# The order of the last two multiplications in a rational activation on Trainium2

## The chip, the cores and the metric

The kernel runs on one core of a Trainium2 chip. The core has five engines that run side by side, each taking its own instructions in order: TensorE (matmuls, PE in the profile, with its weight loads as PEld), VectorE (DVE), ScalarE (ACT), GpSimd (POOL) and SyncE (SP), which here issues the DMAs. The engines wait for each other by semaphores. Operands lie in SBUF or in PSUM, where the matmuls write; PSUM has eight banks. The metric is the device time of one execution in microseconds, less is better.

## The reference

Three layers, one after the other. The first is a linear attention with a decay: for each of 4 x 8 heads a 48 x 48 state is carried over 768 time steps. Its output, 3072 tokens of 384 numbers, goes through two feed-forward layers with 2048 hidden units. The change touches the first of them, whose activation is a rational function of the hidden value h:

```python
h = x @ w_in
h2 = h * h
h3 = h2 * h
P = a[0] + a[1] * h + a[2] * h2 + a[3] * h3
Q = 1.0 + np.abs(b[0]) * np.abs(h) + np.abs(b[1]) * h2
g = P / (Q + 1e-06)
return (g @ w_out).astype(np.float32)
```

The second layer has the same form with `g = h * np.cos(h)`.

## The kernel before, in words

The weights arrive as 64-bit floats and are turned into 32-bit ones on the chip (ScalarE L72 and L73, VectorE L77 and L78). Every matmul operand is split into a high and a low part, and a product takes three passes (high by high, high by low, low by high). The order of the work is written out by hand: the program calls the helpers below in the order in which each engine is to run its instructions.

The first part of the run, up to about 105 us, is the attention, in 24 units. The first feed-forward layer overlaps its end. A tile of that layer is 128 hidden units by 512 tokens, and there are 6 x 16 = 96 tiles. The second layer follows with 32 tiles of the same kind, and then its remaining blocks of tokens by a scheme that saves multiplications (`threes`).

`layers(n)` is one step. It runs, in this order: `gemm1(n)`, nine matmuls of tile n into a PSUM bank (L562); `rational(n)`, one stage each for the four tiles before; `second(n)`, the nine matmuls L578 of the tile five before, which need the split activation; and small pieces of other work: the conversion of weights, and the splitting of the next block's input (`x_lo`, VectorE L706, reads two SBUF tiles). The 18 matmuls of a step take about 4.2 us.

The banks of the hidden values go round: tile n uses bank n mod 4 (`b0`, `b1`, `b2`, `r0`; the profile calls them b and r). So `gemm1(n)` can start only when the last reader of tile n - 4 is done.

`rational(n)` does the following. For tile n - 4 ScalarE rounds g to its high part (L608) and GpSimd subtracts to get the low part (L613). For tile n - 1 ScalarE makes |h| (L636) and a linear function of h (L637), GpSimd makes z = |h| (c1 |h| + c0) in two instructions (L638, L639), and VectorE multiplies g by h (L640). For tile n - 2 VectorE does the next step of the polynomial (L628), and ScalarE computes a first guess r of the reciprocal of the scaled denominator, as exp(-ln(...)), in two instructions (L645, L646) and writes it over h in the tile's PSUM bank. For tile n - 3 VectorE corrects the guess by one Newton step and multiplies (L631 to L633). So VectorE has five instructions a step, in the order L628, L631, L632, L633, L640. Of their large operands z and g lie in SBUF, h and r in PSUM.

Of the kernel before, what the change touches and what calls it, by code (L numbers as in the profile page):

```python
# [15 lines left out]
ALU = mybir.AluOpType  # L16
# [15 lines left out]
LN_S = 2.0 ** -22  # L32
# [10 lines left out]
def attn_then_two_moe(ctx, tc, kqT, aT, vP, w1i, w1o, ma, mb, w2i, w2o, out):  # L43
    nc = tc.nc
# [51 lines left out]
    def temp(tag, dtype=F32, shape=(128, TB)):  # L96

        bufs = {"z": 3, "ah": 2, "g": 4, "hi": 3, "lo": 3}[tag]
        return el.tile(list(shape), dtype, tag=tag, name=tag, bufs=bufs)
# [486 lines left out]
    def acc_out(most=NK):  # L586

        while outs and most:
            most -= 1
            m, blk, f, k = outs.pop(0)  # L590
            ks = slice(k * 128, (k + 1) * 128)
            if f < NF - 1:
                nc.scalar.activation(out=part(blk, k), in_=acc[k], func=AF.Copy)
                continue
            o = temp("z" if k == 1 else "g") if m or blk == NC - 1 else in_p.tile([128, TB], F32, tag="p", name="o")
            if in_parts(m, blk):
                nc.vector.tensor_tensor(out=o, in0=part(blk, k), in1=acc[k], op=ALU.add)
            elif m == 1 and k == 1 and blk in (0, NC - 1):
                nc.vector.tensor_copy(o, acc[k])
            else:  # L600
                nc.scalar.activation(out=o, in_=acc[k], func=AF.Copy)
            to = xd[1][blk, ks, :] if m == 0 else out[ks, blk * TB:(blk + 1) * TB]
            nc.sync.dma_start(out=to, in_=o)

    def round_g(n):
        t = T[n]
        t["hi"] = temp("hi", F32R)
        nc.scalar.activation(out=t["hi"], in_=t["g"], func=AF.Copy)  # L608

    def rest_g(n, eng):  # L610
        t = T[n]
        t["lo"] = temp("lo", F32R)
        eng.tensor_tensor(out=t["lo"], in0=t["g"], in1=t["hi"].bitcast(F32), op=ALU.subtract)  # L613

    def rational(n):

        def tile_at(i):
            return T[i] if 0 <= i < N1 else None

        one, two, three, four = (tile_at(n - i) for i in range(1, 5))  # L620
        acc_out(1)
        if four:
            round_g(n - 4)
            rest_g(n - 4, nc.gpsimd)
        acc_out()
        if two:
            g = two["g"]
            nc.vector.scalar_tensor_tensor(g, g, cq[:, 3:4], two["h"], ALU.add, ALU.mult)  # L628
        if three:
            z, r, g = three["z"], three["h"], three["g"]  # L630
            nc.vector.scalar_tensor_tensor(z, z, ONE_EPS, r, ALU.add, ALU.mult)  # L631
            nc.vector.scalar_tensor_tensor(r, z, -2.0 / LN_S, r, ALU.add, ALU.mult)  # L632
            nc.vector.scalar_tensor_tensor(g, g, cq[:, 2:3], r, ALU.add, ALU.mult)  # L633
        if one:
            h, ah, g, zz = one["h"], temp("ah"), temp("g"), temp("z")
            nc.scalar.activation(out=ah, in_=h, func=AF.Abs)  # L636
            nc.scalar.activation(out=g, in_=h, func=AF.Identity, scale=cq[:, 5:6], bias=cq[:, 4:5])  # L637
            nc.gpsimd.tensor_scalar(zz, ah, cq[:, 1:2], cq[:, 0:1], ALU.mult, ALU.add)  # L638
            nc.gpsimd.tensor_tensor(out=zz, in0=zz, in1=ah, op=ALU.mult)  # L639
            nc.vector.tensor_tensor(out=g, in0=g, in1=h, op=ALU.mult)  # L640
            one.update(z=zz, g=g)
        if two:

            r = two["h"]
            nc.scalar.activation(out=r, in_=two["z"], func=AF.Ln, scale=LN_S, bias=lnb)  # L645
            nc.scalar.activation(out=r, in_=r, func=AF.Exp, scale=-1.0)  # L646
# [581 lines left out]
    def layers(n):  # L1228
# [12 lines left out]
        elif n < 2 * NF:  # L1241
            at, load = n - 2 * NF + 4, n == 2 * NF - 6
        split = 0 <= at < NK and nxt[0] < 2 and nxt != (1, 2)
        rational(n)
        cosine_parts(n)
        cosine(n)
# [280 lines left out]
```

## Time and profile before

| What | us |
|---|---|
| median of three runs (913.3 to 915.9) | 914.39 |
| the profiled execution | 913.8 |
| its span, first to last instruction | 912.1 |
| TensorE matmuls busy | 892.4 |
| TensorE weight loads busy | 741.2 |
| GpSimd busy | 702.9 |
| ScalarE busy | 697.1 |
| VectorE busy | 693.9 |

The granted TensorE clock was 0.996 of full speed over the span. Shares of busy time are averages over stages; the table of stages below tells more. An instruction's record runs from its start to its end, and when it is held up after its start by something other than a semaphore, the record becomes longer. In the chain of work that ended last TensorE has 72%, VectorE 8%, ScalarE 7% and GpSimd 6%.

### The profile page before, as it was taken

The numbers are of one execution on the slowest core, as the hardware profiler recorded it, in microseconds if no ns is written. First come the engines' busy times: TensorE is split into PE (matmuls) and PEld (weight loads), VectorE is DVE, ScalarE is ACT, GpSimd is POOL, SyncE is SP. The second block draws the span as 40 slices with busy tenths as digits, with TensorE's granted clock in tenths as the row PEclk, the third lists the DMA queues.
The fourth block names the chain that finished last, engine by engine and source line by source line (L and its number), as shares of the span: only waits on it lengthen the run. The fifth ranks groups of instructions, "written<-read, shape, count | busy, mean of one in ns | idle before, by whom it ended". The sixth has DMA issues, their size and how long they took to land.

```text
span 912.1 us, 16494 instructions
## 1 busy us (share of the span) xinstructions
PE 892.4 (98%) x5732; PEld 741.2 (81%) x5732; DVE 693.9 (76%) x1247; ACT 697.1 (76%) x1302; POOL 702.9 (77%) x699
## 2 busy tenths in 40 slices
PE   7999999999999999999999999999999999999997
PEld 7788777887788888888888888878888888888885
DVE  7989799998999989989979767666366554555552
ACT  5999898989889788888788778656577666666653
POOL 6899998999889888889879668669787475655332
PEclk9999999999999999999999999999999999999999
DMA  8999545211233141232165276630243433533432
GB/s 281 357 366 370 191 124 196 82 63 36 104 107 94 57 142 45 87 107 94 53 205 185 95 238 239 202 110 27 74 134 109 161 113 96 167 102 105 139 105 90
DMA packets 67307, 128.87 MB, mean 141 GB/s; under 512 B 6928, under 2 KB 30224, under 8 KB 67216
## 3 DMA queue, kind: packets, MB, share of 16 engines
q1 hardware_dynamic: 67216, 127.74, 43.1%
q8 instruction: 47, 0.77, 0.4%
q14 instruction: 44, 0.36, 0.1%
HBM read 95.21 MB, written 32.51 MB: 140 GB/s over the span
## 4 chain that ended last, share of the span: by engine, by line
PE 72%; DVE 8%; ACT 7%; POOL 6%; DMA 4%; issue 2%; SPq 0%; DVEq 0%; ACTq 0%
PE acc L578 22%; PE b L562 18%; PE acc L1054 15%; PE b L1019 6%; PE r L1019 5%; PE r L562 4%; POOL kq L323 2%; POOL kq L318 2%; DMA kq<-kqT 2%; DVE g L628 1%; DVE z L631 1%; ACT b L645 1%; DVE g L640 1%; DMA a<-aT 1%; PE b L1198 1%
## 5 line engine op out<-in xcount | busy, mean ns | idle before, releaser
L578 PE MATMUL acc<-hi,w 128*128 128x512 f32 x738 | 252.5, 396 | 0.0
L562 PE MATMUL b<-x,w 128*128 128x512 f32 x927 | 233.8, 397 | 1.3 <-DVE g L633 1.1
L613 POOL TENSOR_TENSOR lo<-g,hi 128x512 fp32r<-128x512 f32 x128 | 170.2, 1330 | 66.2 <-ACT hi L608 59.4
L562 PEld LDWEIGHTS b<-x,w 128*128 128x128 f32 x927 | 173.4, 188 | 45.4 <-DVE g L633 4.1
L578 PEld LDWEIGHTS acc<-hi,w 128*128 128x128 f32 x738 | 138.7, 188 | 33.9
L1111 POOL TENSOR_TENSOR lo<-g,hi 128x512 fp32r<-128x512 f32 x64 | 83.0, 1297 | 103.6 <-ACT hi L1110 91.6
L578 PE MATMUL acc<-lo,w 128*128 128x512 f32 x369 | 145.7, 395 | 0.0
L639 POOL TENSOR_TENSOR z<-z,ah 128x512 f32<-128x512 f32 x96 | 124.7, 1299 | 8.0
L1054 PE MATMUL acc<-hi,w_out 128*128 128x512 f32 x384 | 130.3, 395 | 0.0
L608 ACT ACTIVATE hi<-g 128x512 fp32r<-128x512 f32 x128 | 80.4, 628 | 47.8 <-PE acc L578 32.6
L578 PEld LDWEIGHTS acc<-lo,w 128*128 128x128 f32 x369 | 69.4, 188 | 16.5
L638 POOL TENSOR_SCALAR z<-ah,cq 128x512 f32<-128x512 f32 x96 | 74.4, 775 | 5.5 <-ACT ah L636 5.4
L1054 PE MATMUL acc<-lo,w_out 128*128 128x512 f32 x192 | 76.4, 398 | 0.4 <-POOL lo L1111 0.2
L1054 PEld LDWEIGHTS acc<-hi,w_out 128*128 128x128 f32 x384 | 68.7, 188 | 9.9
L640 DVE TENSOR_TENSOR g<-g,b 128x512 f32<-128x512 f32 x72 | 49.1, 682 | 16.2 <-ACT g L637 16.0
L636 ACT ACTIVATE ah<-b 128x512 f32<-128x512 f32 x72 | 42.8, 594 | 19.9 <-PE b L562 19.6
L562 PE MATMUL r<-x,w 128*128 128x512 f32 x225 | 56.8, 397 | 1.0 <-DVE g L633 1.0
L1096 DVE SCALAR_TENSOR_TENSOR ah<-z,b 128x512 f32<-128x512 int32 x44 | 30.2, 685 | 35.9 <-ACT z L1092 35.9
L637 ACT ACTIVATE g<-b,cq 128x512 f32<-128x512 f32 x72 | 56.1, 779 | 0.0
L633 DVE SCALAR_TENSOR_TENSOR g<-g,cq,b 128x512 f32<-128x512 f32 x72 | 53.9, 748 | 2.5
L628 DVE SCALAR_TENSOR_TENSOR g<-g,cq,b 128x512 f32<-128x512 f32 x72 | 53.4, 742 | 0.5
L645 ACT ACTIVATE b<-z,lnb 128x512 f32<-128x512 f32 x72 | 50.1, 696 | 4.7 <-DVE g L628 4.0
(202 smaller groups left out, 2028.7 us busy)
## 6 DMA issues: line engine op xcount, KB each, us to landing
w_out<-wd SPq DMA_DIRECT2D x64, 384.0 KB, 3.1
kq<-kqT SPq DMA_DIRECT2D x24, 512.0 KB, 6.6
w<-wd SPq DMA_DIRECT2D x16, 384.0 KB, 3.1
wd<-w SPq DMA_DIRECT2D x16, 384.0 KB, 2.6
a<-aT SPq DMA_DIRECT2D x23, 258.0 KB, 5.8
raw<-w2o SPq DMA_DIRECT2D x14, 384.0 KB, 3.9
v<-vP SPq DMA_DIRECT2D x24, 192.0 KB, 6.6
x<-x1d SPq DMA_DIRECT2D x18, 256.0 KB, 4.2
```

What stands on the lines that cost most here:

```text
L562: nc.tensor.matmul(h, ws[0][f][:, w, ks], x[:, xx, kk, :], start=i == 0, stop=i == 8)
L578: nc.tensor.matmul(acc[k], ws[1][f][:, w, ks], d[g], start=first and i == 0, stop=last and i == 2)
L608: nc.scalar.activation(out=t["hi"], in_=t["g"], func=AF.Copy)
L613: eng.tensor_tensor(out=t["lo"], in0=t["g"], in1=t["hi"].bitcast(F32), op=ALU.subtract)
L628: nc.vector.scalar_tensor_tensor(g, g, cq[:, 3:4], two["h"], ALU.add, ALU.mult)
L638: nc.gpsimd.tensor_scalar(zz, ah, cq[:, 1:2], cq[:, 0:1], ALU.mult, ALU.add)
L639: nc.gpsimd.tensor_tensor(out=zz, in0=zz, in1=ah, op=ALU.mult)
L640: nc.vector.tensor_tensor(out=g, in0=g, in1=h, op=ALU.mult)
L645: nc.scalar.activation(out=r, in_=two["z"], func=AF.Ln, scale=LN_S, bias=lnb)
L1019: nc.tensor.matmul(tile[:, half], w[p], x[q], start=start and i == 0, stop=True, skip_group_check=True)
L1054: nc.tensor.matmul(acc[k], item["w"][:, w, ks], item[g], start=first, stop=last)
L1111: nc.gpsimd.tensor_tensor(out=p["lo"], in0=p["g"], in1=p["hi"].bitcast(F32), op=ALU.subtract)
```

## The change

For tile n - 3 the order of the last two multiplications is exchanged. Before: z becomes (z + 1.000001) r, then r becomes (z - 2/c) r, the corrected reciprocal, and then g becomes (g + c2) r. After: z as before, then g becomes (g + c2) r with the uncorrected guess, and last g becomes (z - 2/c) g. The product is the same up to rounding. r is no longer written by VectorE.

```diff
         if three:
             z, r, g = three["z"], three["h"], three["g"]
             nc.vector.scalar_tensor_tensor(z, z, ONE_EPS, r, ALU.add, ALU.mult)
-            nc.vector.scalar_tensor_tensor(r, z, -2.0 / LN_S, r, ALU.add, ALU.mult)
             nc.vector.scalar_tensor_tensor(g, g, cq[:, 2:3], r, ALU.add, ALU.mult)
+            nc.vector.scalar_tensor_tensor(g, z, -2.0 / LN_S, g, ALU.add, ALU.mult)
```

## Rows read from the trace of the kernel before

**Rows 1.** Busy time by stage: window, length, then each engine's busy us.
```profile
110.00:135.00 25.00, 22.70 (x170) 17.45 (x169) 21.35 (x34) 22.54 (x44) 23.13 (x24) 1.00 0.47 138
135.00:210.00 75.00, 74.88 (x320) 59.42 (x319) 71.54 (x115) 68.74 (x130) 69.59 (x65) 1.00 0.33 104
210.00:245.00 35.00, 33.86 (x143) 26.20 (x142) 32.67 (x51) 29.43 (x53) 31.91 (x29) 1.00 0.19 58
245.00:510.00 265.00, 265.00 (x1138) 213.50 (x1136) 240.86 (x368) 221.27 (x391) 231.31 (x208) 1.00 0.35 112
510.00:912.00 402.00, 395.49 (x2133) 336.62 (x2131) 233.06 (x439) 261.67 (x503) 247.79 (x253) 1.00 0.40 127
```

**Rows 2.** Waits of TensorE for VectorE: total us, times, longest us.
```profile
PE b L562 <- DVE g L633: 1.1, 2, 0.7
PE r L562 <- DVE g L633: 1.0, 1, 1.0
```

**Rows 3.** Timeline, two of these waits: start, us, instruction, idle before, releaser.
```profile
132.46 1.90 PE L562 MATMUL r<-x,w 128*128 128x512 f32 x7 [0.96 <-DVE g L633]
...
226.63 1.67 PE L562 MATMUL b<-x,w 128*128 128x512 f32 x6 [0.67 <-DVE g L633]
```

**Rows 4.** Timeline, two steps of the second stage.
```profile
161.05 0.70 DVE L632 SCALAR_TENSOR_TENSOR b<-z,b 128x512 f32<-128x512 f32 x1
161.05 1.30 POOL L613 TENSOR_TENSOR lo<-g,hi 128x512 fp32r<-128x512 f32 x1
...
161.78 0.75 DVE L633 SCALAR_TENSOR_TENSOR g<-g,cq,b 128x512 f32<-128x512 f32 x1
...
162.81 2.26 PE L562 MATMUL b<-x,w 128*128 128x512 f32 x9
...
164.77 1.30 POOL L613 TENSOR_TENSOR lo<-g,hi 128x512 fp32r<-128x512 f32 x1 [0.28 <-ACT hi L608]
...
165.61 0.75 DVE L633 SCALAR_TENSOR_TENSOR g<-g,cq,r 128x512 f32<-128x512 f32 x1
```

**Rows 5.** VectorE's groups by form: count, busy us, mean ns, idle before.
```profile
L633 DVE SCALAR_TENSOR_TENSOR g<-g,cq,b 128x512 f32<-128x512 f32 x72 | 53.9, 748 | 2.5
...
L632 DVE SCALAR_TENSOR_TENSOR b<-z,b 128x512 f32<-128x512 f32 x72 | 50.1, 696 | 2.5
```

**Rows 6.** Lines L706 and L632 alone: duration in ns, least, median, most.
```profile
L706 DVE TENSOR_TENSOR x<-x x21: 683/733/1333, 127.4 to 566.8; 128x512 fp32r<-128x512 f32 x21
...
L632 DVE SCALAR_TENSOR_TENSOR b<-z,b x72: 695/696/698, 116.2 to 512.6; 128x512 f32<-128x512 f32 x72
```

**Rows 7.** Timeline, VectorE and GpSimd around an L318 and an L706.
```profile
107.56 1.27 POOL L639 TENSOR_TENSOR z<-z,ah 128x512 f32<-128x512 f32 x1
...
108.12 1.26 DVE L318 TENSOR_TENSOR kq<-kq,z 128x512 f32<-128x512 f32 x1
...
108.79 1.46 POOL L225 TENSOR_TENSOR w<-st,w 128x384 fp32r<-128x384 f32 x1
...
287.47 1.30 POOL L639 TENSOR_TENSOR z<-z,ah 128x512 f32<-128x512 f32 x1
...
288.01 1.31 DVE L706 TENSOR_TENSOR x<-x 128x512 fp32r<-128x512 f32 x1
...
288.73 1.77 POOL L613 TENSOR_TENSOR lo<-g,hi 128x512 fp32r<-128x512 f32 x1
```

**Rows 8.** GpSimd's groups between 245 and 510 us: count, busy us, mean ns.
```profile
L613 POOL TENSOR_TENSOR lo<-g,hi 128x512 fp32r<-128x512 f32 x64 | 85.7, 1338 | 23.5 <-ACT hi L608 17.0 <-PE acc L578 6.5
L639 POOL TENSOR_TENSOR z<-z,ah 128x512 f32<-128x512 f32 x64 | 83.2, 1299 | 5.3
L638 POOL TENSOR_SCALAR z<-ah,cq 128x512 f32<-128x512 f32 x64 | 49.5, 773 | 5.5 <-ACT ah L636 5.4
L225 POOL TENSOR_TENSOR v<-st,kq 128x384 fp32r<-128x384 f32 x16 | 16.4, 1023 | 0.7
```

## The prediction

> **What bounds the kernel now.** I read the stages first [rows 1]. From 110 us on TensorE is busy 22.70 of 25 us, 74.88 of 75, 33.86 of 35 and 265.00 of 265; the tiles that the change touches run in these four stages, at some 4.2 us a step, which makes about 18, 8 and 64 steps of the last three. So the end is set by TensorE's matmuls, and the change can move it only by opening or closing gaps between them. The gaps there sum to 2.30 + 0.12 + 1.14 = 3.56 us. Next the waits of TensorE [rows 2]: of those gaps 1.1 + 1.0 = 2.1 us, in three waits, end with L633, the last of the four instructions in which VectorE finishes a tile and with it frees the PSUM bank that the tile's reciprocal lies in. The timeline has the two longest, 0.96 us at 132.46 and 0.67 us at 226.63 [rows 3].
>
> The same stage rows show how little room the helpers have: VectorE is busy 71.54 of 75 us in the second stage, GpSimd 69.59. TensorE is full there because the helpers just keep pace: at 162.81 the matmuls of a new tile start [rows 4], 0.28 us after L633 of the tile that held their bank (161.78 + 0.75 = 162.53). That 0.28 us is all the cover there is at that point.
>
> **The change part by part.** No instruction is added or removed and none goes to another queue; every step still has five on VectorE. The third to come changes from "r = (z - 2/c) r" to "g = (g + c2) r", the old L633, and the fourth from that to "g = (z - 2/c) g".
>
> *The third.* L632 took 0.696 us, L633 0.748 [rows 5], so it is 0.05 longer in its new place, and it is now the last to read the bank. The bank comes free at 0.748 in place of 0.696 + 0.03 (start to start 0.73, rows 4) + 0.748 after L631's end: about 0.7 us sooner. That is worth at most the three waits, each cut by up to 0.7: 0.7 + 0.67 + 0.4 = 1.8 us.
>
> *The fourth.* Before, all five had one operand in PSUM (h or r). The new fourth has z and g, both in SBUF. The trace has no SCALAR_TENSOR_TENSOR of that kind, so I bound it by the VectorE instructions that do read two SBUF tiles. L706 (128x512, both in SBUF) takes 0.683 us at best, 0.733 in the median and 1.333 at worst [rows 6]. At best it is level with L632's 0.696: nothing is gained by leaving PSUM. Why the worst is twice as long can be read off the timeline [rows 7]: L706 at 288.01 finds GpSimd inside L639, which ends at 287.47 + 1.30 = 288.77; L706 ends at 289.32, 0.55 us after that. L318 at 108.12 finds L639 until 108.83 and ends at 109.38, again 0.55 later. And GpSimd pays too: the instruction issued meanwhile, L613 at 288.73, takes 1.77 us against its usual 1.30 (0.47 more), L225 at 108.79 takes 1.46 against 1.02. So on this chip a VectorE instruction with two SBUF inputs waits until the running GpSimd instruction has ended, and the next GpSimd instruction then waits for it. The new fourth costs w + 0.55 us, w being what is left of the GpSimd instruction it meets, and GpSimd 0.47 us.
>
> The Trainium skill (SBUF — State Buffer, "Who interferes with whom") says the same of the port that the two engines share: a VectorE instruction with two SBUF inputs contends with a GpSimd instruction that reads SBUF, and the one that comes second blocks fully. By its wording, that the pair is held for the whole instruction, GpSimd would lose some 0.7 us a step in place of the rows' 0.47, and the second stage alone would lose 4 us more; the rows decide.
>
> *How large w is.* GpSimd's instructions between 245 and 510 us [rows 8] give, for an arrival at a random moment, the sum of count times length squared over twice the stage: (64 x 1.338^2 + 64 x 1.299^2 + 64 x 0.773^2 + 16 x 1.023^2) / 530 = 0.52 us. The two steps shown in the second stage agree: L633 starts with 0.57 us of L613 left at 161.78 and 0.46 left at 165.61 [rows 4]. Bounds are 0 (GpSimd idle) and 1.3 (a long one just begun); I take 0.52. VectorE's step then grows by 0.52 + 0.55 - 0.70 = 0.37 us, GpSimd's by 0.47. Behind the waiting fourth stand, on VectorE, L640 of the youngest tile, a weight conversion if one is due, and L628 and L631 of the next step: so a late fourth makes the next bank late as well, unless VectorE has idle time to win it back. ScalarE (L608) and GpSimd (L613) need its g too, but their products are wanted only a step or more later, so that this wait alone costs nothing.
>
> *By stage* [rows 1]:
> - 110 to 135: the 0.96 us wait shrinks by 0.7, with VectorE idle 3.65 us: -0.7.
> - 135 to 210, 18 steps: VectorE's idle time is 3.46/18 = 0.19 us a step, GpSimd's 5.41/18 = 0.30. Both are overdrawn, VectorE by 0.18 and GpSimd by 0.17. Some of that idle time is the 0.03 us between dependent instructions and can't be used, so I take 0.2: 18 x 0.2 = 3.6, less the cover of 0.28 + 0.7 us: +2.6.
> - 210 to 245, 8 steps with three L706 of their own: idle 2.33/8 = 0.29 on VectorE and 3.09/8 = 0.39 on GpSimd, against 0.37 and 0.47 more. Overdrawn by 0.08, with the same allowance about 0.15, in a stage where TensorE waits already: +1.2.
> - 245 to 510, 64 steps: idle 24.14/64 = 0.38 on VectorE, 33.69/64 = 0.53 on GpSimd. The additions just fit on average. They don't fit where twelve L706 and the weights' conversions crowd (the stage begins without cover); I take 12 crowded steps overdrawn by 0.2: +2.4.
> - after 510: no such steps; TensorE's order is unchanged: 0.
>
> Sum +5.5 us on the profiled execution's 913.8 (its span 912.1 and 1.7 around it): 919.3. That execution lies 0.6 under the median of 914.4, so I say 919.9.
>
> **Rivals.**
> *The new fourth does not wait* (912.6). If the contention belongs to TENSOR_TENSOR alone, which is the operation of every two-SBUF row, the fourth costs 0.69 at any time, VectorE's step is unchanged, and only the sooner bank is left: -1.8. It decides at each of the 96 new fourths, and is right if they take about 0.69 us with GpSimd running. For it: no row shows the operation itself. Against: L706 and L318 come from different tiles and stages and end 0.55 after GpSimd alike, which looks like the port and not the operation.
>
> The skill's sentence speaks of inputs, not of an operation, though the operations it lists by name do not include this one.
>
> *The wait is real but goes where there is room* (915.3). In the last long stage TensorE's pace, not VectorE's, sets the phase once VectorE is ahead; a late fourth slides to the end of GpSimd's instruction and then meets a short remainder. With w at 0.15 or less VectorE pays nothing, GpSimd's 0.47 fits in 0.53 there, and the overdraft of 135 to 245 is GpSimd's alone, 18 x 0.17 + 8 x 0.08 = 3.7 us, of which the cover of 1.0 and the 1.8 of the saved waits leave 0.9. Against it: between 135 and 245 there is no such room.
>
> *The two engines fall into a bad lock* (near 936). If VectorE meets a fresh long instruction step after step, w is 1.3 and a step grows by 1.15 us against 0.38 idle: 0.77 x 64 = 49 us in the last stage if it lasts. It can't last long, since each such wait moves VectorE later against GpSimd by the time it waited; a third of the steps gives 16 us on top of mine, 936.
>
> **How the numbers follow.** Forecast (slower by 3 to 12 us) 0.58, no waiting 0.14, absorbed 0.18, bad lock 0.10. A difference under 0.3%, 2.7 us, can't be told from none. The two middle cases fall almost wholly within it; I give 0.03 of them to a gain over it (more than the 1.8 of the waits, from gaps the trace puts to others) and move 0.02 of the forecast into it: faster 0.03, same 0.31, slower 0.66. The range takes in the no-wait case and reaches up until about one in ten is left: 912 to 931.
>
> **What would show it.** Right: the new fourth on VectorE with a mean near 1.05 us and a spread from 0.69 to 1.85, no longer all alike as L632 was (0.695 to 0.698) [rows 6]; L638, L639 or L613 lengthened by up to 0.47; VectorE's and GpSimd's busy time up by some 35 and 30 us; the waits of TensorE for L633 gone or shorter at 132 us, and new ones for VectorE between 150 and 300. Wrong: the fourth flat at 0.69 (then the first rival), or lengthened as said with TensorE as full as before from 245 on and no gaps before it (then the second). The time itself refutes me under 917 or over 931.

## The result and the profile after

The changed kernel takes 920.86 us (median of four, 920.16 to 923.73), the kernel before 914.27; the ratio is 1.0076, with a 95% interval of 1.0050 to 1.0102. So it is slower by 0.8%, 6.6 us, where 919.9 was forecast.

The profiled execution is the longest of the four: 923.73 us, with a span of 922.0. Its first tile starts 1.80 us late, at 100.88 in place of 99.08, before any instruction that the change touches. What the change costs is read from that tile on. About 1 us of what it loses before 120 us goes with a fall of the granted clock (last section).

First the stages, as in [rows 1].

```profile
110.00:135.00 25.00, 23.49 (x185) 18.46 (x181) 21.51 (x31) 21.47 (x42) 23.80 (x22) 0.93 0.43 123
135.00:210.00 75.00, 71.61 (x298) 54.52 (x297) 74.28 (x105) 63.52 (x119) 69.70 (x58) 1.00 0.33 104
210.00:245.00 35.00, 33.17 (x137) 24.66 (x136) 33.55 (x51) 31.05 (x58) 33.89 (x29) 1.00 0.12 35
245.00:510.00 265.00, 264.59 (x1134) 212.91 (x1133) 253.01 (x367) 220.88 (x387) 258.20 (x207) 1.00 0.34 109
```

Read the counts in brackets behind TensorE's busy time. Between 135 and 210 us it got through 298 matmuls, before through 320. Nine take 2.10 us, so 22 fewer is 5.1 us lost in that stage alone. The next stage lost 6 (1.4 us), the long one 4 (0.9 us). VectorE has become full in the second stage, 74.28 of 75. In the long stage GpSimd went from 231.31 to 258.20 and VectorE from 240.86 to 253.01, and TensorE hardly noticed.

The starts of single tiles tell the same without gaps in the counts. These are TensorE's rows in the timeline of the changed kernel.

```profile
100.88 2.36 PE L562 MATMUL b<-x,w 128*128 128x512 f32 x9
...
134.76 1.09 PE L562 MATMUL r<-x,w 128*128 128x512 f32 x4
...
217.21 2.37 PE L562 MATMUL b<-x,w 128*128 128x512 f32 x9 [0.22 <-DVE g L632]
...
253.95 2.36 PE L562 MATMUL b<-x,w 128*128 128x512 f32 x9 [0.41 <-DVE g L632]
...
522.85 2.26 PE L562 MATMUL b<-x,w 128*128 128x512 f32 x9
```

The same tiles of the kernel before start at 99.08, 132.46, 209.01, 244.60 and 513.50. The lag is 1.80, 2.30, 8.20, 9.35 and 9.35 us. Nearly all of it, 5.9 us, is built up between 135 and 217 us, and none in the 270 us after 254.

Now VectorE's two instructions and GpSimd's three, whole run, as in [rows 5, 8].

```profile
L633 DVE SCALAR_TENSOR_TENSOR g<-z,g 128x512 f32<-128x512 f32 x96 | 100.8, 1050 | 3.3
...
L632 DVE SCALAR_TENSOR_TENSOR g<-g,cq,b 128x512 f32<-128x512 f32 x72 | 53.3, 740 | 0.0
...
L613 POOL TENSOR_TENSOR lo<-g,hi 128x512 fp32r<-128x512 f32 x128 | 181.1, 1415 | 40.9 <-ACT hi L608 40.9
L639 POOL TENSOR_TENSOR z<-z,ah 128x512 f32<-128x512 f32 x96 | 131.0, 1365 | 8.0
L638 POOL TENSOR_SCALAR z<-ah,cq 128x512 f32<-128x512 f32 x96 | 99.8, 1039 | 0.0
```

The new fourth instruction, L633, has a mean of 1.050 us where the old L632 had 0.696. On GpSimd L638 went from 0.775 to 1.039, L639 from 1.299 to 1.365, L613 from 1.330 to 1.415. The timeline of the second stage shows how. First column the start, second the duration.

```profile
161.77 1.29 POOL L613 TENSOR_TENSOR lo<-g,hi 128x512 fp32r<-128x512 f32 x1
162.42 1.19 DVE L633 SCALAR_TENSOR_TENSOR g<-z,g 128x512 f32<-128x512 f32 x1
163.04 1.21 POOL L638 TENSOR_SCALAR z<-ah,cq 128x512 f32<-128x512 f32 x1
...
166.57 1.29 POOL L613 TENSOR_TENSOR lo<-g,hi 128x512 fp32r<-128x512 f32 x1
166.62 1.79 DVE L633 SCALAR_TENSOR_TENSOR g<-z,g 128x512 f32<-128x512 f32 x1
167.85 1.21 POOL L638 TENSOR_SCALAR z<-ah,cq 128x512 f32<-128x512 f32 x1
...
170.66 1.29 POOL L613 TENSOR_TENSOR lo<-g,hi 128x512 fp32r<-128x512 f32 x1 [0.21 <-ACT hi L608]
171.42 1.08 DVE L633 SCALAR_TENSOR_TENSOR g<-z,g 128x512 f32<-128x512 f32 x1
171.93 1.21 POOL L638 TENSOR_SCALAR z<-ah,cq 128x512 f32<-128x512 f32 x1
```

Each L633 meets L613 and ends 0.55 us after it: 161.77 + 1.29 = 163.06, and 162.42 + 1.19 = 163.61. Each L638 behind it takes 1.21 in place of 0.77 and ends 0.64 us after L633 (163.04 + 1.21 = 164.25). This is the pattern of L318 and L706 [rows 7] with another operation. The three remainders of GpSimd's instruction that they meet, 0.64, 1.24 and 0.53 us, come back every third step until 231 us.

Last the waits of TensorE (total, times, longest), as in [rows 2].

```profile
PE b L562 <- DVE g L632: 3.4, 10, 0.8
...
PE acc L578 <- POOL w L225: 1.2, 1, 1.2
PE r L562 <- DVE g L632: 0.7, 2, 0.3
```

Twelve short waits for a bank stand where three did, though the instruction that frees it comes earlier in the step, and one matmul waits for a weight that GpSimd finished late.

### The profile page after: what moved, and what is told of

Read it like the earlier page. It is cut to its first block, busy times and chain, and to the rows that moved or that the text cites. A ratio compares the mean times of both kernels' runs of the same rounds, so it can differ in the third digit from the quotient of the medians.

```text
span 922.0 us, 16494 instructions
## 1 busy us (share of the span) xinstructions
PE 895.3 (97%) x5732; PEld 739.9 (80%) x5732; DVE 721.0 (78%) x1247; ACT 700.0 (76%) x1302; POOL 744.7 (81%) x699
## 4 chain that ended last, share of the span: by engine, by line
PE 75%; DVE 12%; POOL 5%; ACT 3%; issue 2%; DMA 2%; DVEq 0%; ACTq 0%; SPq 0%
PE acc L578 22%; PE b L562 18%; PE acc L1054 15%; PE b L1019 6%; PE r L1019 5%; PE r L562 4%; DVE g L633 2%; DVE g L628 2%; DVE g L632 2%; DVE g L640 2%; POOL kq L318 2%; POOL kq L323 2%; DVE z L631 2%; DMA kq<-kqT 1%; PE b L1198 1%
## 5 line engine op out<-in xcount | busy, mean ns | idle before, releaser
L562 PE MATMUL b<-x,w 128*128 128x512 f32 x927 | 234.7, 397 | 3.6 <-DVE g L632 3.4
L613 POOL TENSOR_TENSOR lo<-g,hi 128x512 fp32r<-128x512 f32 x128 | 181.1, 1415 | 40.9 <-ACT hi L608 40.9
L562 PEld LDWEIGHTS b<-x,w 128*128 128x128 f32 x927 | 172.7, 188 | 50.3 <-DVE g L632 9.2
L1111 POOL TENSOR_TENSOR lo<-g,hi 128x512 fp32r<-128x512 f32 x64 | 83.1, 1299 | 103.5 <-ACT hi L1110 91.5
L639 POOL TENSOR_TENSOR z<-z,ah 128x512 f32<-128x512 f32 x96 | 131.0, 1365 | 8.0
L633 DVE SCALAR_TENSOR_TENSOR g<-z,g 128x512 f32<-128x512 f32 x96 | 100.8, 1050 | 3.3
L638 POOL TENSOR_SCALAR z<-ah,cq 128x512 f32<-128x512 f32 x96 | 99.8, 1039 | 0.0
L562 PE MATMUL r<-x,w 128*128 128x512 f32 x225 | 57.6, 400 | 0.7 <-DVE g L632 0.7
L640 DVE TENSOR_TENSOR g<-g,b 128x512 f32<-128x512 f32 x72 | 48.7, 677 | 6.9 <-ACT g L637 6.9
L632 DVE SCALAR_TENSOR_TENSOR g<-g,cq,b 128x512 f32<-128x512 f32 x72 | 53.3, 740 | 0.0
```

What stands on the lines that cost most here:

```text
L562: nc.tensor.matmul(h, ws[0][f][:, w, ks], x[:, xx, kk, :], start=i == 0, stop=i == 8)
L633: nc.vector.scalar_tensor_tensor(g, z, -2.0 / LN_S, g, ALU.add, ALU.mult)
L1111: nc.gpsimd.tensor_tensor(out=p["lo"], in0=p["g"], in1=p["hi"].bitcast(F32), op=ALU.subtract)
```

## The experiments

Where a tile's lag is given it is against the kernel before, from the start of TensorE's L562, and tiles go by their start in the kernel before. The texts that were put down before each run call the runs by numbers. In the order below these are e1, e2, e3, e4, e5 with its repetitions e11 and e12, e6 and e7, e9 and e10, and e8.

**The new order without two SBUF inputs.**

```diff
-            nc.vector.scalar_tensor_tensor(g, g, cq[:, 2:3], r, ALU.add, ALU.mult)
-            nc.vector.scalar_tensor_tensor(g, z, -2.0 / LN_S, g, ALU.add, ALU.mult)
+            nc.vector.scalar_tensor_tensor(r, g, cq[:, 2:3], r, ALU.add, ALU.mult)
+            nc.vector.scalar_tensor_tensor(g, z, -2.0 / LN_S, r, ALU.add, ALU.mult)
```

> The new order of the two multiplications is kept, but (g + c2) r goes into r's PSUM bank, so that the last multiplication reads z from SBUF and r from PSUM, as every VectorE instruction of the step did before. Theory (two SBUF inputs make VectorE wait for GpSimd and GpSimd for VectorE): the time of the kernel before, 914.3 within 1.5 us; L633 flat near 0.70 us, L638 back at 0.77. Rival (the order itself costs, for instance because g is finished later for ScalarE): 920.9, as the changed kernel.

Measured: 913.43 us, ratio to the kernel before 0.999 (0.998 to 1.000). L633 and L638, least, median and most:

```profile
L633 DVE SCALAR_TENSOR_TENSOR g<-z,b x72: 686/686/691, 117.4 to 512.2; 128x512 f32<-128x512 f32 x72
...
L638 POOL TENSOR_SCALAR z<-ah,cq x96: 764/776/807, 107.2 to 508.2; 128x512 f32<-128x512 f32 x96
```

The order costs nothing. With one operand in PSUM the fourth instruction is flat and GpSimd is back.

**The old order with two SBUF inputs.**

```diff
-            nc.vector.scalar_tensor_tensor(r, z, -2.0 / LN_S, r, ALU.add, ALU.mult)
-            nc.vector.scalar_tensor_tensor(g, g, cq[:, 2:3], r, ALU.add, ALU.mult)
+            nc.vector.scalar_tensor_tensor(z, z, -2.0 / LN_S, r, ALU.add, ALU.mult)
+            nc.vector.scalar_tensor_tensor(g, g, cq[:, 2:3], z, ALU.add, ALU.mult)
```

> The old order is kept (the corrected reciprocal first, g last), but the corrected reciprocal is written over z in SBUF, so that the last multiplication has two SBUF inputs, z and g. Theory: the time of the changed kernel, 920.9 within 1.5 us, with L633 at a mean near 1.05 us. Rival (the order costs): 914.3.

Measured: 924.21 us, ratio 1.0114 (1.0098 to 1.0130). All of the loss is back with the old order, and 3.3 us more.

```profile
L633 DVE SCALAR_TENSOR_TENSOR g<-g,cq,z 128x512 f32<-128x512 f32 x96 | 103.7, 1080 | 3.4
```

Its shortest case is 0.751 against 0.691 in the changed kernel; 0.06 us more in each of the 26 steps between 135 and 245 would be 1.6 of the 3.3, an estimate that no run tests. Another 1.0 us is two waits of TensorE for L632 between 245 and 290. The two runs together show that the operands' place decides and not the order. They don't clear the bank: in the first of them r is read until the fourth instruction, as before, and in the second the bank comes free after the third, as in the changed kernel. The next run does.

**The fourth instruction left out.**

```diff
             nc.vector.scalar_tensor_tensor(g, g, cq[:, 2:3], r, ALU.add, ALU.mult)
-            nc.vector.scalar_tensor_tensor(g, z, -2.0 / LN_S, g, ALU.add, ALU.mult)
```

> The last multiplication by (z - 2/c) is left out, so the guess of the reciprocal stays uncorrected; VectorE has four instructions a step and the bank comes free as soon as in the changed kernel. What the sooner bank and an idle VectorE can give at most: the waits of TensorE for VectorE vanish, 1.8 to 2.5 us, so 911.8 to 912.5. If the slower time had to do with the bank or with the first three instructions, it would stay near 920.

Measured: 910.39 us, ratio 0.9958 (0.9945 to 0.9971), 3.9 us under the kernel before, more than expected. Between 135 and 245 TensorE is busy 75.00 of 75 and 35.00 of 35 us. So neither the sooner bank nor the first three instructions make the changed kernel slower. How much of the gain is the bank's is not shown, since VectorE also has an instruction less; in the run below that relieves VectorE and leaves the bank as before, the gain is 2.4 us.

**Early or late tiles only.**

```diff
-            nc.vector.scalar_tensor_tensor(g, g, cq[:, 2:3], r, ALU.add, ALU.mult)
-            nc.vector.scalar_tensor_tensor(g, z, -2.0 / LN_S, g, ALU.add, ALU.mult)
+            if n - 3 < 30:
+                nc.vector.scalar_tensor_tensor(g, g, cq[:, 2:3], r, ALU.add, ALU.mult)
+                nc.vector.scalar_tensor_tensor(g, z, -2.0 / LN_S, g, ALU.add, ALU.mult)
+            else:
+                nc.vector.scalar_tensor_tensor(r, z, -2.0 / LN_S, r, ALU.add, ALU.mult)
+                nc.vector.scalar_tensor_tensor(g, g, cq[:, 2:3], r, ALU.add, ALU.mult)
```

> The new order for the first 30 of the 96 tiles alone (up to about 250 us), the old one after. From the ladder of start times in the changed kernel, all of the loss is there although only 30 of 96 new instructions are: theory 920.9 within 1 us. Rival, by my own sum (2.4 of its 5.5 us after 245 us, or in proportion to the instructions that pay): 918.5, or 914.3 + 6.6 x 30/96 = 916.4.

Measured: 920.82 us, ratio 1.0078 (1.0064 to 1.0091): the changed kernel's time to 0.1 us, with 30 of its 96 new instructions. Its profile has a granted clock of 1.00 from 110 to 245 us, so that its tiles show the cost without the fall of the clock that the changed kernel's profile has.

```profile
98.03 2.36 PE L562 MATMUL b<-x,w 128*128 128x512 f32 x9
...
130.25 2.33 PE L562 MATMUL r<-x,w 128*128 128x512 f32 x9
...
213.33 2.36 PE L562 MATMUL b<-x,w 128*128 128x512 f32 x9 [0.22 <-DVE g L633]
...
250.03 2.36 PE L562 MATMUL b<-x,w 128*128 128x512 f32 x9 [0.42 <-DVE g L633]
```

Against 99.08, 132.46, 209.01 and 244.60 that is 1.05 and 2.21 us early, then 4.32 and 5.43 late.

For the next runs the condition is turned round, to `n - 3 >= 30`.

> The counterpart of e4: the old order for the first 30 tiles, the new one for the other 66. The 66 new instructions should still wait for GpSimd (mean near 0.99 us) and lengthen GpSimd's work, but TensorE has cover there: 914.3 within 1 us. Rival, loss in proportion to the instructions that pay: 914.3 + 6.6 x 66/96 = 918.8; by my own sum's last term: 916.7.

Measured: 916.55 us, ratio 1.0019 (1.0006 to 1.0033), with a gap in the middle: four of twelve executions took 913.7 to 914.4, eight 916.3 to 919.5. The profiled one was of the short kind. Its 66 new instructions wait as foreseen, and TensorE's tiles keep their times, 0.41 us early at 244.19 and at 513.09.

```profile
L634 DVE SCALAR_TENSOR_TENSOR g<-z,g 128x512 f32<-128x512 f32 x66 | 65.2, 988 | 2.3
```

To catch a long one the same kernel ran twice more.

> The kernel of e5 once more, for a profile of one of its longer executions (eight of twelve took 916.3 to 919.5, four 913.7 to 914.4; the one profiled was of the short kind and lost nothing between 99 and 547 us). If the new instructions of the last long stage cost there at times, TensorE's tiles slip by 2 to 3 us between 245 and 515 us. If they don't, the slip lies before 110 or after 547 us, where nothing of the change runs.

> The kernel of e5 a third time, as e11, since one profile may again be of the short kind: a slip of TensorE's tiles by 2 to 3 us between 245 and 515 us if the late instructions cost at times, none there if they don't.

Measured: 914.11 and 914.92 us, both short. Between 244.6 and 513.5 the lag stays at 0.20 in the one and 0.57 in the other. So no profile shows the late instructions costing anything. The median of the twelve is still 2.1 us above the 914.45 of the kernel before beside it, of whose 26 executions two took over 916, and where the longer executions spend these 2 us stays open.

**GpSimd relieved.** L639 is left out of both kernels, so z is not multiplied by |h|.

```diff
-            nc.gpsimd.tensor_tensor(out=zz, in0=zz, in1=ah, op=ALU.mult)
```

> The kernel before without GpSimd's L639 (z is left at c1 |h| + c0, the multiplication by |h| is left out). Base for e7. VectorE stays what paces the second stage, so little changes: 913 to 914.5.

> The changed kernel without GpSimd's L639, as in e6. GpSimd is then busy some 62% in the second stage, a random arrival finds 0.35 us left (18 x (1.30^2 + 0.777^2) + 11 x 1.026^2, over 150), VectorE's step grows by 0.20 against 0.19 idle. Theory that GpSimd's occupancy makes the price: within 1.5 us of e6, L633's mean between 0.8 and 0.95 us. Rival (a lock in which the new instruction meets a fresh L613 every few steps whatever GpSimd's load): e6 + 5 or more, L633's mean at 1.2 in the second stage.

Measured: 916.97 us for the base (ratio 1.0028, 1.0018 to 1.0038) and 916.13 for the changed form (1.0012, 1.0000 to 1.0024). The base is 2.5 us slower than expected. Its profile is already 5.5 us late at the first tile, with a granted clock of 0.50 between 100 and 104 us. The profile of the changed form loses 4.5 us between the tiles of 109.53 and 116.31, 3.5 of them in one wait for ScalarE's L425 that ends at 116.60, before its first new fourth at 119.2; its granted clock is 0.50 between 116 and 120. So the medians alone say little. What holds is what the tiles do from 132.46 to 509.30 us: the base goes from 5.29 to 4.84 us late and the changed form from 3.78 to 1.88. Neither loses anything there: the price is gone. The second stage of the changed form:

```profile
135.00:210.00 75.00, 75.00 (x322) 60.29 (x322) 74.17 (x116) 69.17 (x130) 50.95 (x47) 1.00 0.35 110
```

and its fourth instruction from 135 to 219 us:

```profile
L633 DVE SCALAR_TENSOR_TENSOR g<-z,g 128x512 f32<-128x512 f32 x20 | 18.1, 903 | 0.7
```

Its mean is 0.903, so w is 0.35, as worked out. VectorE is as full as in the changed kernel, but gets through 116 instructions in place of 105, and TensorE is full all the same.

**VectorE relieved.** L640 is left out of both kernels, so the youngest polynomial is not multiplied by h.

```diff
-            nc.vector.tensor_tensor(out=g, in0=g, in1=h, op=ALU.mult)
```

> The kernel before without VectorE's L640 (the multiplication of the youngest tile's polynomial by h is left out). Base for e10: VectorE has some 0.65 us a step more idle time, so that the three waits of TensorE for its banks vanish or shrink: 911.5 to 913.5.

> The changed kernel without VectorE's L640, as in e9. The new multiplication still waits for GpSimd and GpSimd for it. If VectorE's lack of idle time in the second stage is what turns the wait into lost time, VectorE now has 0.19 + 0.65 us idle a step against 0.4 to 0.6 more, and the time is within 1.5 us of e9. If GpSimd's lost 0.45 us a step (against 0.30 idle) paces the stage by itself, e9 + 2 to 3.5. If the wait costs whoever has room or not, e9 + 6.

Measured: 911.75 us for the base (0.9970, 0.9955 to 0.9985) and 918.14 for the changed form (1.0039, 1.0026 to 1.0052): 6.4 apart, the full price. My theory that VectorE's lack of idle time makes the loss fell here, and the time is that of the third case. The second stage of the changed form and a wait of ScalarE between 135 and 245:

```profile
135.00:210.00 75.00, 72.03 (x305) 56.52 (x305) 65.80 (x93) 65.96 (x121) 73.58 (x62) 1.00 0.34 104
```

```profile
ACT b L644 <- POOL z L639: 7.9, 14, 1.7
```

VectorE has 9.2 us idle, but GpSimd is now the full one, 73.58 of 75, and ScalarE waits for its z. One 2.7 us wait of TensorE for a weight of GpSimd's L225 stands in the same profile. The tiles tell where the 6.4 us are lost. Between 132.46 and 209.01 the changed form loses 3.7 us and its base 0.3, so 3.4 are left of the 5.9 that this stretch cost without the relief, most of them that one wait. Between 209.01 and 244.60 it loses another 1.3 where its base gains 1.9. So relief for VectorE did make the second stage cheaper, to the 2 to 3.5 us of the second case, and the next stage took it back; why, was not followed up.

**Another place for the fourth.** It is issued after L640.

```diff
-            nc.vector.scalar_tensor_tensor(g, z, -2.0 / LN_S, g, ALU.add, ALU.mult)
...
             nc.vector.tensor_tensor(out=g, in0=g, in1=h, op=ALU.mult)
             one.update(z=zz, g=g)
+        if three:
+            nc.vector.scalar_tensor_tensor(three["g"], three["z"], -2.0 / LN_S, three["g"], ALU.add, ALU.mult)
```

> The changed kernel with the new multiplication moved behind L640 of the youngest tile, so that it arrives some 0.65 us later in VectorE's step. By the remainders seen in the changed kernel's second stage (0.53, 0.65, 1.24 us of L613 in turn), it then meets L638 with about 0.65, 0.74 and 0.56 us left: mean 0.65 in place of 0.81, 18 x 0.15 = 2.7 us less, 918. If the phase adjusts itself to whatever follows: 921 as the changed kernel. Back to 914 only if the place and not the operands were the cause.

Measured: 920.83 us, ratio 1.0062 (1.0049 to 1.0075), the changed kernel's time. The mean between 135 and 219 us fell to 1.109 us (w 0.56), more than foreseen. By the tiles 4.1 us are lost between 132.46 and 209.01 in place of 5.9, but 2.0 in place of 1.15 from there to 244.60, and the median did not follow. TensorE is 15 matmuls short in the second stage, and one of its waits, for a weight that GpSimd's L225 splits, is 2.1 us long.

```profile
135.00:210.00 75.00, 72.26 (x305) 56.28 (x304) 71.61 (x109) 66.24 (x121) 70.38 (x60) 1.00 0.33 104
```

## Why the prediction was right, and where its sum was not

The mechanism is the one forecast. A VectorE instruction with two SBUF inputs waits for GpSimd's running instruction plus 0.55 us, and GpSimd's next loses 0.44. That holds for SCALAR_TENSOR_TENSOR as for TENSOR_TENSOR, so the first rival (no wait, 912.6) is out; the mean of 1.050 us was forecast as "near 1.05". The two crossed runs, order against operands, show it from both sides.

The 0.55 and the 0.44 us are one rule. Each engine's instruction ends some 0.13 us sooner after the other's than it takes alone, and no more: in the median VectorE's fourth, 0.69 alone, ends 0.55 after the GpSimd instruction that it meets; L638, 0.775 alone, ends 0.65 after the fourth, and L613, 1.30 alone, 1.16 after it. The Trainium skill (SBUF — State Buffer, "Who interferes with whom") says that the engine that comes second blocks fully. Up to these 0.13 us the trace agrees, for both engines. The 0.7 us a step that the prediction worked out from that wording left them out; the rows' 0.47 are no evidence against the wording.

The total came out within 1 us because terms of the sum missed in opposite directions, and that is luck. So is part of the mean: 1.050 is an average of 1.285 in one stage and 0.989 in another. GpSimd's busy time rose by 42 us and not by some 30; 96 times the prediction's own 0.47 would have been 45.

- *135 to 210 us: +2.6 forecast, some 5.9 measured, 6.5 where only the early tiles have the new order.* The mis-sized term is w. I took 0.52 us for an arrival at a random moment and found it confirmed by two steps. Between 135 and 210 us the fourth has a mean of 1.285 us, so w is 0.74: VectorE and GpSimd locked into a cycle of three steps, and each third step met an L613 that had just begun. That is the third rival in a mild form, where the cover is least. With 0.74 the same working gives 0.74 + 0.55 - 0.70 - 0.19 = 0.40 us a step, 7.2 in all, 6.2 after the cover of 1.0. That the sum then fits does not show that w alone makes the loss: with VectorE relieved, 3.4 us of it stay.

```profile
L633 DVE SCALAR_TENSOR_TENSOR g<-z,g 128x512 f32<-128x512 f32 x17 | 21.8, 1285 | 0.6
```

- *245 to 510 us: +2.4 forecast, 0 measured.* Here w is 0.44 (mean 0.989 from 254 to 519 us). VectorE's step grew by 12.2/64 = 0.19 us and GpSimd's by 26.9/64 = 0.42, inside their idle 0.38 and 0.53. That the crowded steps would overdraw it was wrong (only the old order with two SBUF inputs, whose instruction is longer, lost 1.0 us there); the second rival had the outcome of this stage right, though not its w of 0.15.
- *210 to 245 us: +1.2 forecast.* The tiles give 9.35 - 8.20 = 1.15 from 217 to 254 us.
- *110 to 135 us: -0.7 forecast, -1.2 measured.* In the changed kernel's own profile the wait of 0.96 us is gone, but the tile after it is 0.5 us later; its granted clock was 0.93 there against 1.00 before. Where only the early tiles have the new order, at a clock of 1.00, the lag goes from -1.05 at the first tile to -2.21 at this one. The bank's worth was put too low.

Of the two overdrafts that I had side by side, GpSimd's weighs more than I gave it. Relief for VectorE left the total as it was, relief for GpSimd took the price away: the less GpSimd has to do, the smaller w is (0.35), and where VectorE has 9.2 us to spare, GpSimd's 0.44 us a step still make TensorE wait. Leaving L639 out also gives ScalarE its z sooner, so that this pair doesn't separate the two fully.

No version here that computes the whole function beats both kernels clearly. The new order through PSUM is at 0.999 (0.998 to 1.000).

## What to carry to other kernels

Before an elementwise chain is reordered, look where each operand of each VectorE instruction lies: a PSUM operand, even one that seems a detour, keeps it out of GpSimd's way. Price an instruction with two SBUF inputs on both engines, the remainder it meets on VectorE and about half a microsecond on GpSimd, stage by stage against the idle time there; the remainder can lock to a bad phase, so test it at more than the mean. When a sum over stages comes out right, check its terms, for here errors of 3.3 and 2.4 us nearly cancelled.

## What the runs showed of the hardware

That the operands' place gives nothing back was not a given: a fourth that meets no GpSimd instruction takes 0.691 us with both inputs in SBUF and 0.686 with one in PSUM.

The granted clock fell in some executions just before the first changed tile, the profiled one of the changed kernel among them. Between 116 and 120 us:

```profile
116.00:120.00 4.00, 3.77 (x34) 3.17 (x35) 3.93 (x7) 3.97 (x9) 3.92 (x5) 0.65 0.50 159
```

The granted clock is 0.65 of full speed there, so that a part of the four microseconds ran at the lower of its levels, 1.2 and 2.4 GHz. This is just where TensorE had waited 1.51 us for ScalarE's L425; the kernel before shows 1.00 in the same four microseconds, though it had waited 1.34 us for the same line. Without the fourth instruction, with it in another place and in the first repetition of the late tiles the four microseconds have 0.73, 0.62 and 0.69, with the early tiles alone 1.00. So the fall comes with and without the new fourth, and what sets it off is not shown. The changed kernel's tiles slipped by 1.06 us across it: two of them start at 111.32 and 119.16 us, before at 109.53 and 116.31.
